# First decay rows copied inside SBUF, VectorE columns and residues in other instructions, and a split copy of the last tile

## The chip, the core and the metric

The kernel runs on one core of a Trainium2 chip. The metric is the device time of one execution in microseconds. Five engines run side by side, each with its own queue of instructions in a fixed order: TensorE (PE; PEld is its weight load), VectorE (DVE), ScalarE (ACT), GpSimd (POOL) and SyncE (SP), which here only issues DMAs. An instruction waits until the semaphores that it needs are set, and what stands behind it on its engine waits with it.

## The reference

```python
# 1. attention with decay: B, H, S, D = 4, 8, 576, 64
scores = scale * np.matmul(q, k.transpose(0, 1, 3, 2))
cum = np.cumsum(np.log(np.clip(f, 0.0001, 1.0)), axis=-1)
scores = np.where(causal, -1000000000.0, scores + cum[:, :, :, None] - cum[:, :, None, :])
attn = softmax(scores); x = attn @ v                # -> (4, 576, 512)
# 2. mixture of 4 attention experts, top 2 by gate
logits = x @ w_gate
for e in range(4):
    q, k, v = x @ wq[e], x @ wk[e], x @ wv[e]
    ye = softmax(causal(scale * q @ k.T)) @ v @ wo[e]
    out += gate(logits, e) * ye
# 3. mixer: u = x + (x^T U V)^T, and a hidden layer of 2048
u = x + h.transpose(0, 2, 1)                         # h = x^T @ U @ V
return u + np.maximum(u @ w_ch1, 0.0) @ w_ch2
```

U, V, w_ch1 and w_ch2 come as 64-bit floats.

## The kernel before

The host only lays the arrays out. The order of the instructions is made while the program is written: each piece of work is a generator that asks for an engine, a buffer or an event, and a greedy planner (class Plan, with planned costs and the priorities PR) always runs the piece that can begin first. Each engine then executes its queue in that order, whatever the true times are. A change of a planned cost, or one more step, can so change the order of all that follows. The DMAs of the program use eight semaphores in turn (DMAHW0 to DMAHW7 in the order's rows): a DMA waits until the one before it on its semaphore has landed.

**Layer 1.** Keys and queries of one head stand in a buffer Y (three buffers). Four more partitions, 64 to 67, hold rows made of the decay sums, so that one f32 matmul gives score plus decay. decay() reads f, takes Ln on ScalarE, sums with a scan on VectorE and splits the sums into two parts (the region rw of w2x, rows of 576). It writes six rows a head to DRAM (aug), 8 heads first, then 24; rows() reads them back into Y for each head. The first heads turn the exponentials with TensorE transposes (into the PSUM banks hid and mm) and copy them out on ScalarE and VectorE (pt); later ones split P into an f16 part and an f16 residue (parts()) and turn them by DMA. A residue is x - hi: on VectorE by one instruction, on GpSimd by another; the planner chooses.

**Scales.** Each tensor is scaled by a power of two. pow2() gets the largest power not above the maximum, as a column of one element on 128 partitions; scales() makes from it the scale s (a reciprocal) and its inverse; times() multiplies columns. These columns all lie in one tile, cols.

**While layer 1 starts,** SP reads wall (weights of layer 2), U, V and w_ch1, w_ch2. The 64-bit words are turned into f32 (x, sg, w2x). fold() multiplies wo into w_ch1 on TensorE in 16 steps (hid<-x,wtr).

**Layer 3.** hidden() makes relu(z w) for 256 rows and 256 columns a step (hid, g), outputs() adds g w_ch2 for two tiles of 128 rows into acc (two PSUM banks, one tile of the program), store() scales a tile with ScalarE into o, which has one buffer (r_o), and SP writes it out:

```python
        o = yield r_o
        yield "act"
        copy_scaled(o, a, iv)
        ...
        yield "sp"
        r_o.free(o, dma(out[t0:t0 + 128, :], o).t)
```

Of the kernel before, what the change touches and what calls it, by code (L numbers as in the profile page):

```python
# [20 lines left out]
KB = 5  # L21
# [14 lines left out]
QUEUE = ('act', 'act', 'sp', 'act')  # L36
ACTDMA = 100
PEN = 30.0
WINDOW = 10240 / 3
# [203 lines left out]
def attn_moe_mixer(ctx: ExitStack, tc: tile.TileContext, qk, v, f, wall, wot, wo, w1, w2, u3, v3, out):  # L243
# [74 lines left out]
    def ts(out_, in_, s1, op0, s2=None, op1=None, rate=0.55):  # L318
        kw = {} if op1 is None else {"op1": op1}
        dve("tensor_scalar", rate=rate, out=out_, in0=in_, scalar1=s1, scalar2=s2, op0=op0, **kw)  # L320

    def tt(out_, a, b, op):
        dve("tensor_tensor", out=out_, in0=a, in1=b, op=op)
# [46 lines left out]
    def scales(name, e, k):  # L370
        s, si = col(f"s_{name}"), col(f"i_{name}")
        ts(si, e, float(2.0 ** -k), ALU.mult)
        recip(s, si)
        return s, si

    def times(name, *xs):
        t = col(name)
        tt(t, xs[0], xs[1], ALU.mult)
        for x in xs[2:]:
            tt(t, t, x, ALU.mult)  # L380
        return t
# [87 lines left out]


    def load_heads():
        for i, key in enumerate(HEADS):
            kind, b, h = key
            if i == 2:
                yield ev("rows of first")
            if kind == 1:
                HY[key] = yield r_Y
                HG[key] = (HY[key],)
                yield QUEUE[1]
                n = count(2, "loaded", key)  # L480
                n.done(dma(HY[key][0:64], qk[b, h].rearrange("t d s -> d t s"), queue(1)).t)
                spawn(rows(n, b * H + h, HY[key]), 0)
            else:
                yield ev("stg", b, h // 2)
                X = yield r_X.of([128, 3, 576], F16, "Xh")
                stg = STG[b, h // 2][64 * (h % 2):64 * (h % 2) + 64]
                HG[key] = (X, X)
                n = count(3, "loaded", key)

                for to, of in ((X[0:64], stg[:, 1:4]), (X[64:128, 1:3], stg[:, 2:4]), (X[64:128, 0], stg[:, 0])):  # L490
                    yield "sp"
                    n.done(dma(to, of).t)
                if h % 2:
                    spawn(stg_free(b, h), 0)
# [6 lines left out]
    def rows(n, i, Y):  # L501
        yield ev("aug", i // H)
        yield ev("rows", id(Y))
        yield QUEUE[0]
        a = aug[i]
        n.done(dma(Y[64:68], bass.AP(tensor=a.tensor, offset=a.offset, ap=[[S, 4], [2 * S, 2], [1, S]]), queue(0)).t)
        if i == 0:
            ev("rows of first").done()
# [133 lines left out]
    def parts(hi, lo, x):  # L642
# [5 lines left out]
        if (yield Any(dve=170 + 1.04 * n, pool=180 + 1.93 * n)) == "dve":  # L648
            tt(lo, x, hi, ALU.subtract)
        else:  # L650
# [61 lines left out]
    def pv_out(kind, b, p, j, bank, pv):  # L712
# [13 lines left out]
        if kind == 2:  # L726
            yield ev("gate", b)
            yield "dve"
            tt(rr, rr, GATE[b][:, :, h], ALU.mult)
            if count(E, "gated", b).n == 1:  # L730
# [114 lines left out]
    def values_gates(b):  # L845
# [44 lines left out]
        yield "dve"  # L890
        tt(gt, gt, eq, ALU.add)
# [4 lines left out]
        tt(lg, lg, top.to_broadcast([128, KB, 4]), ALU.subtract)  # L896
        yield "act"
# [9 lines left out]
        yield "dve"  # L907
        tt(lg, lg, top.to_broadcast([128, KB, 4]), ALU.mult)
        wq = yield r_wq
# [323 lines left out]
    def outputs():  # L1233
        yield ev("wox")
        for b, g in groups:
# [16 lines left out]
            for n in range(8):  # L1252
                yield ev("g", (b, g, n))
                gh, gl = GV.pop((b, g, n))
                for fi in range(2):
                    f_ = 2 * n + fi
                    yield ev("w2", f_)
                    for t in range(2):
                        ts_ = slice(t * 128, t * 128 + 128)
                        yield "pe"  # L1260
                        mm(acc[t], gh[:, fi, ts_], w2s[:, f_, 0, :], False, False)
                        mm(acc[t], gh[:, fi, ts_], w2s[:, f_, 1, :], False, False)
                        mm(acc[t], gl[:, fi, ts_], w2s[:, f_, 0, :], False, f_ == NF - 1)
                r_g[0].free(gh)
                r_g[1].free(gl)
            for t in range(2):
                spawn(store(b, g, t, both, acc[t]), PR['store'])

    def store(b, g, t, both, a):
        off = 64 * b  # L1270
        z0 = g * 256 + t * 128
        yield ev("iv", b)
        iv = IV[b] if z0 >= off else IV[b - 1] if z0 + 128 <= off else IV[b, "mixed"]
        o = yield r_o
        yield "act"
# [8 lines left out]
        t0 = b * 576 - off + z0  # L1284
        yield "sp"
# [3 lines left out]
    def decay():  # L1289
        rw = w2x[:32, 8:17, :].rearrange("p a n -> p (a n)")[:, :8 * S].rearrange("p (r s) -> p r s", s=S)  # L1290
        rr = rw.bitcast(F32R)
        one, ff_, cum = rw[:, 0], rw[:, 6], rw[:, 7]
        yield "sp"
        got = dma(ff_, f)
        yield "dve"
        for r, x in ((0, 1.0), (4, -1.0)):
            nc.vector.memset(rw[:, r:r + 2], x)
            plan.cost += 700
        yield got
        yield "dve"  # L1300
# [147 lines left out]
```

## Time and profile before

| | |
|---|---|
| median of 3 runs | 770.49 us (770.06 to 771.51) |
| span of the profiled execution | 770.45 us (770.5 on the page) |
| PE busy | 680.5 us, 88% |
| DVE busy | 476.2 us, 62% |
| ACT busy | 424.1 us, 55% |
| POOL busy | 231.3 us, 30% |
| mean granted TensorE clock | 0.974 |

The span is that of one execution, from its first to its last instruction; it agrees with the median. The busy times of engines run side by side, so they don't add up. A matmul or a copy on the path counts fully, work beside it not at all.

### The profile page before, as it was taken

The page shows a single profiled execution, that of the slowest core. Times are in us where ns is not written, and L with a number is a line of the kernel's source. Part 1 is how long each engine was busy: PE and PEld are TensorE (multiplying, and loading weights), DVE is VectorE, ACT ScalarE, POOL GpSimd, SP SyncE. Part 2 cuts the span into 40 slices and gives each one's busy share as a digit, 9 for nine tenths or more (in the row PEclk, how much of TensorE's full clock was granted, in tenths as well). Part 3 has the DMA queues.
Part 4 walks back from the last instruction along what each step waited for, and adds up shares of the span by engine and source line. Part 5 has one row for each costly group of instructions (what it writes and reads, how often), then busy time and mean ns, then how long its engine had stood idle before and what let it go on. Part 6 is the DMA issues. An engine that isn't in the chain of part 4 may idle for free.

```text
span 770.5 us, 15644 instructions
## 1 busy us (share of the span) xinstructions
PE 680.5 (88%) x5810; PEld 466.3 (61%) x5810; DVE 476.2 (62%) x1548; ACT 424.1 (55%) x889; POOL 231.3 (30%) x286
## 2 busy tenths in 40 slices
PE   3767898687788999999999989998899999899996
PEld 2556776565555666666566666665667656565653
DVE  5888899999878645666874365668734753111111
ACT  4757798687776843566765254767633562112111
POOL 4124333450447620344433022554410340000000
PEclk9969999799999999999999999999999999999999
DMA  8645457572276742779896249888762770000000
GB/s 222 183 109 134 131 151 200 162 212 50 67 152 126 134 92 47 159 160 166 153 187 127 52 87 188 149 150 163 134 106 51 142 149 19 27 1 28 1 28 27
DMA packets 195135, 89.14 MB, mean 116 GB/s; under 512 B 163700, under 2 KB 183156, under 8 KB 195028
## 3 DMA queue, kind: packets, MB, share of 16 engines
q1 hardware_dynamic: 179572, 72.89, 45.2%
q10 hardware_dynamic: 15488, 15.27, 7.6%
q8 instruction: 45, 0.74, 0.4%
q14 instruction: 30, 0.25, 0.1%
HBM read 35.68 MB, written 5.16 MB: 53 GB/s over the span
## 4 chain that ended last, share of the span: by engine, by line
PE 50%; DVE 22%; ACT 9%; issue 5%; DMA 3%; POOL 3%; ACTq 1%; SPq 0%; DVEq 0%; POOLq 0%
PE acc L261 18%; PE mm L261 16%; PE hid L261 12%; DVE sc L272 5%; PE sp L261 3%; DMA pt<-P 3%; ACT sc L266 3%; DVE pt L272 2%; DVE cols L272 2%; POOL P L284 2%; DVE P L272 2%; ACT P L266 2%; DVE w2x L272 1%; DVE nm L272 1%; DVE rr L272 1%
## 5 line engine op out<-in xcount | busy, mean ns | idle before, releaser
L261 PE MATMUL acc<-w2x,g 128*128 128x512 f16 x768 | 180.3, 379 | 0.0
L284 POOL TENSOR_TENSOR P<-sc,P 128x576 f16<-128x576 f32 (+4 forms) x148 | 115.1, 790 | 202.1 <-ACT P L266 154.7
L261 PEld LDWEIGHTS <-g 128*128 128x128 f16 x864 | 82.7, 98 | 83.9 <-issue 1.0
L266 ACT ACTIVATE sc<-sc,nm 128x576 f32<-128x576 f32 (+4 forms) x190 | 103.2, 556 | 47.8 <-DVE nm L272 44.0
L272 DVE SCALAR_TENSOR_TENSOR g<-hid,g 128x512 f16<-128x512 f32 x72 | 49.6, 689 | 122.8 <-ACT g L266 122.5
L261 PE MATMUL sp<-Y 128*128 128x320 f32 (+4 forms) x344 | 106.7, 424 | 17.1 <-DVE nm L272 10.6
L261 PE MATMUL hid<-z,wfr 128*128 128x256 f16 x864 | 107.7, 273 | 5.8 <-DVE g L272 4.7
L261 PEld LDWEIGHTS <-wfr 128*128 128x128 f16 x864 | 83.7, 98 | 30.1 <-issue 8.9
L266 ACT ACTIVATE g<-hid 128x512 f16<-128x512 f32 x72 | 42.6, 591 | 104.9 <-PE acc L261 76.2
L261 PEld LDWEIGHTS sp<-Y 128*128 128x128 f32 x344 | 57.4, 195 | 47.5 <-DVE nm L272 31.2
L266 ACT ACTIVATE P<-sc 128x320 f16<-128x320 f32 (+4 forms) x164 | 70.3, 457 | 20.3 <-DMA pt<-P 10.2
L261 PE MATMUL mm<-V,pt 128*128 128x65 f16 x2058 | 74.5, 194 | 0.8 <-DVE xn L272 0.4
L261 PEld LDWEIGHTS <-pt 128*128 128x128 f16 x2058 | 70.1, 98 | 2.2 <-DVE xn L272 0.7
L261 PE MATMUL mm<-xt,wall 128*128 128x288 f16 x384 | 52.7, 291 | 2.2 <-DVE stg L272 1.9
L272 DVE CUSTOM_DVE_ANT_0 sc<-sp,mask 128x288 f32<-128x288 f32 (+4 forms) x110 | 45.8, 427 | 9.3 <-POOL P L284 5.7
L261 PE MATMUL hid<-x,wtr 128*128 128x128 f32 x256 | 40.2, 323 | 7.2 <-POOL x L284 4.0
L261 PEld LDWEIGHTS <-wall 128*128 128x128 f16 x384 | 37.9, 99 | 13.3 <-issue 2.5
L284 POOL TENSOR_TENSOR xh<-xn,xh 128x320 f16<-128x320 f32 x31 | 27.4, 885 | 58.8 <-ACT xh L266 56.2
L261 PEld LDWEIGHTS hid<-x,wtr 128*128 128x128 f32 x256 | 37.5, 233 | 10.1 <-POOL x L284 5.9
L261 PE MATMUL sp<-Xh 128*128 128x64 f16 (+2 forms) x192 | 33.1, 284 | 10.9 <-DVE nm L272 9.9
L272 DVE CUSTOM_DVE_ANT_0 sc<-sp,mask,cols 64x64 f32<-64x64 f32 (+4 forms) x80 | 38.6, 489 | 6.4 <-POOL P L284 3.1
L284 POOL TENSOR_TENSOR x<-x,sg 128x512 f32<-128x512 f32 (+2 forms) x19 | 23.1, 1217 | 64.5 <-DVE x L272 54.7
(141 smaller groups left out, 997.5 us busy)
## 6 DMA issues: line engine op xcount, KB each, us to landing
wd<-in_w SPq DMA_DIRECT2D x32, 512.0 KB
Y<-in_qk ACTq DMA_DIRECT2D x32, 288.0 KB
vr<-in_v ACTq DMA_DIRECT2D x16, 320.0 KB
out_dram<-o SPq DMA_DIRECT2D x18, 256.0 KB
Xh<-stg SPq DMA_DIRECT2D x16, 216.0 KB
Xh<-stg SPq DMA_DIRECT2D x16, 144.0 KB
w2x<-in_wall SPq DMA_DIRECT2D x4, 386.0 KB
Xh<-stg SPq DMA_DIRECT2D x16, 72.0 KB
```

Of the source, the lines that this page charges most:

```text
L261: nc.tensor.matmul(out_, lhsT=lhsT, rhs=rhs, start=start, stop=stop, **kw)
L266: nc.scalar.activation(out_, in_, fn, **kw)
L272: getattr(nc.vector, op)(**kw)
L284: getattr(nc.gpsimd, op)(out=out_, **kw)
```

## The change

Five edits:

- rows(): for the first three heads (DIRECT) the decay rows go from the region rw straight to Y, by two DMAs a head of four rows each, with no DRAM between. The other heads read aug as before.
- decay(): a column of ones gets a Ln before f is there, and an Exp behind the real Ln, each with its own table load.
- scales(): s is made by integer arithmetic on the exponent, in one tensor_scalar, ahead of its inverse; the reciprocal goes. times() multiplies by columns given as scalars, two in one instruction.
- parts() and four other places (the gates): a difference or product of two tensors on VectorE is written as scalar_tensor_tensor (times 1.0 first) in place of tensor_tensor.
- outputs() and store(): in the last step of the last group the matmuls of the first tile stand ahead of those of the second, and the first is stored at once. The second is copied in two halves, ScalarE's and VectorE's, into the buffer sc, and each half has its own DMA.

```diff
+DIRECT = 3
+    def stt(out_, a, b, op):
+        dve("scalar_tensor_tensor", out=out_, in0=a, scalar=1.0, in1=b, op0=ALU.mult, op1=op)
     def scales(name, e, k):
         s, si = col(f"s_{name}"), col(f"i_{name}")
+        ts(s.bitcast(I32), e.bitcast(I32), -1.0, ALU.mult, float((254 + k) << 23), ALU.add)
         ts(si, e, float(2.0 ** -k), ALU.mult)
-        recip(s, si)
         return s, si
     def times(name, *xs):
         t = col(name)
-        tt(t, xs[0], xs[1], ALU.mult)
-        for x in xs[2:]:
-            tt(t, t, x, ALU.mult)
+        ts(t, xs[0], xs[1], ALU.mult, *((xs[2], ALU.mult) if len(xs) > 2 else ()))
+        for x in xs[3:]:
+            ts(t, t, x, ALU.mult)
         return t
...
     def rows(n, i, Y):
-        yield ev("aug", i // H)
+        direct = i < DIRECT
+        yield ev("cum") if direct else ev("aug", i // H)
         yield ev("rows", id(Y))
-        yield QUEUE[0]
-        a = aug[i]
-        n.done(dma(Y[64:68], bass.AP(tensor=a.tensor, offset=a.offset, ap=[[S, 4], [2 * S, 2], [1, S]]), queue(0)).t)
+        if direct:
+            for t in range(2):
+                yield QUEUE[0]
+                n.done(dma(Y[64:68, t], CUM[0][i:i + 1, 2 * t:2 * t + 4], queue(0)).t)
+        else:
...
         if (yield Any(dve=170 + 1.04 * n, pool=180 + 1.93 * n)) == "dve":
-            tt(lo, x, hi, ALU.subtract)
+            residue(lo, x, hi)
...
-                for fi in range(2):
+                end = (b, g) == groups[-1] and n == 7
+                for i in range(4):
+                    fi, t = (i % 2, i // 2) if end else (i // 2, i % 2)
...
+                    if end and i == 1:
+                        spawn(store(b, g, t, both, acc[t]), PR['store'])
...
     def store(b, g, t, both, a):
...
+        if (b, g) == groups[-1] and t == 1:
+            o = (yield r_sc[KB - 1])[:, :DM]
+            for engine, to, cs in (("act", nc.scalar, slice(0, DM // 2)), ("dve", None, slice(DM // 2, DM))):
+                yield engine
+                if engine == "act":
+                    copy_scaled(o[:, cs], a[:, cs], iv)
+                else:
+                    ts(o[:, cs], a[:, cs], iv, ALU.mult)
+            for to, cs in ((None, slice(DM // 2, DM)), (nc.scalar, slice(0, DM // 2))):
+                yield "act" if to else "sp"
+                dma(out[t0:t0 + 128, cs], o[:, cs], to)
+            return
...
     def decay():
+        warm = col("warm", 2)
...
+        nc.vector.memset(warm, 1.0)
...
+        yield "act"
+        act(warm[:, 0:1], warm[:, 0:1], ACT.Ln)
         yield got
         yield "dve"
         ts(ff_, ff_, 1e-4, ALU.max, 1.0, ALU.min)
         yield "act"
         act(ff_, ff_, ACT.Ln)
+        yield "act"
+        act(warm[:, 1:2], warm[:, 1:2], ACT.Exp)
...
+        CUM.append(rw)
+        ev("cum").done()
```

At the start of the program ScalarE's queue stood like this before (vr are the values of layer 1, junk the output of an Abs whose sum is kept, sc_97 to sc_99 the first three blocks of the first head, Y_94 to Y_96 the buffers of the first three heads):

```order
L292 DMA vr<-in_v 128x5x128
L266 ACT_TABLE_LOAD
L266 ACTIVATE w2x<-w2x 32x576 [waits DVE_49]
L266 ACTIVATE junk,cols<-vr 128x640 [waits DMAHW3_49]
L266 ACTIVATE junk,cols<-vr 128x640 [waits DMAHW5_49,Activation_49]
L292 DMA Y_94<-aug 4x2x576 [waits DMAHW6_49,DMAHW0_49,Pool_49]
L292 DMA Y_95<-aug 4x2x576 [waits DMAHW1_49,Pool_49]
L292 DMA Y_96<-in_qk 64x2x576 [waits DMAHW2_49]
```

And now, from the read of the second values to the first exps and the copy of U (x<-wd):

```order
L267 ACT_TABLE_LOAD
L267 ACTIVATE cols<-cols 128x1
L267 ACTIVATE junk,cols<-vr 128x640 [waits DMAHW3_49]
L293 DMA Y_94<-w2x 4x1x576 [waits DVE_49,Pool_49]
L293 DMA Y_95<-w2x 4x1x576 [waits DMAHW0_49,Pool_49]
L293 DMA Y_94<-w2x 4x1x576 [waits DMAHW1_49]
L293 DMA Y_95<-w2x 4x1x576 [waits DMAHW2_49]
L267 ACTIVATE junk,cols<-vr 128x640 [waits DMAHW5_49,Activation_49]
L293 DMA Y_96<-w2x 4x1x576 [waits DMAHW6_49]
L267 ACTIVATE sc_97<-sp,nm 64x64 [waits DVE_49]
L267 ACTIVATE sc_98<-sp,nm 128x192 [waits DVE_49]
L267 ACTIVATE x<-wd 128x480 [waits DMAHW7_49]
```

The row DMAs moved ahead of the second Abs, they are two for each head, and the copy of U, which waits for its DMA, stands ahead of the exp of sc_99.

SP's queue, just behind its first two reads, went like this before (aug<-w2x are the DRAM writes of the decay rows, w2x<-in_wall the weights of layer 2, wd<-in_u the read of U):

```order
L292 DMA aug<-w2x 8x3456 [waits DVE_49]
L292 DMA aug<-w2x 24x3456
L292 DMA w2x<-in_wall 128x772 [waits DMAHW3_49]
L292 DMA w2x<-in_wall 128x772 [waits DMAHW4_49]
L292 DMA w2x<-in_wall 128x772 [waits DMAHW6_49]
L292 DMA w2x<-in_wall 128x772 [waits DMAHW7_49]
L292 DMA wd<-in_u 128x960 [waits DMAHW0_49]
```

And now:

```order
L293 DMA aug<-w2x 8x3456 [waits DVE_49]
L293 DMA aug<-w2x 24x3456 [waits DMAHW5_49]
L293 DMA wd<-in_u 128x960 [waits DMAHW7_49]
L293 DMA wd<-in_v 96x576 [waits DMAHW0_49]
L293 DMA w2x<-in_wall 128x772 [waits DMAHW1_49]
```

U moved ahead of the weights; its semaphore DMAHW7 was last used by the first of the two DRAM writes, and DMAHW5 by the second values.

At the end of the program TensorE's last step went, in its middle, like this before (g_9590 and g_9591 are the two parts of the last relu; the first three matmuls shown are the first tile's, the others the second's):

```order
L261 MATMUL acc<-w2x,g_9590 128x512
L261 LDWEIGHTS g_9590
L261 MATMUL acc<-w2x,g_9590 128x512
L261 LDWEIGHTS g_9591
L261 MATMUL acc<-w2x,g_9591 128x512
L261 LDWEIGHTS g_9590
L261 MATMUL acc<-w2x,g_9590 128x512
```

And now, where the first tile's six matmuls are over with the third row and the second tile's begin (the relu's parts are g_9588 and g_9589 here):

```order
L262 MATMUL acc<-w2x,g_9588 128x512
L262 LDWEIGHTS g_9589
L262 MATMUL acc<-w2x,g_9589 128x512
L262 LDWEIGHTS g_9588
L262 MATMUL acc<-w2x,g_9588 128x512 [waits Activation_49]
L262 LDWEIGHTS g_9588
```

The wait for ScalarE in front of the second tile is new. ScalarE ended with these rows before:

```order
L266 ACTIVATE g_9558<-hid 128x512 [waits DVE_49,PE_49]
L266 ACTIVATE g_9574<-hid 128x512 [waits DVE_49,PE_49]
L266 ACTIVATE g_9590<-hid 128x512 [waits DVE_49,PE_49]
L266 ACTIVATE o<-acc,cols 128x512 [waits DMAHW0_49,PE_49]
L266 ACTIVATE o<-acc,cols 128x512 [waits DMAHW1_49,Activation_49]
```

And now:

```order
L267 ACTIVATE g_9572<-hid 128x512 [waits DVE_49,PE_49]
L267 ACTIVATE g_9588<-hid 128x512 [waits DVE_49,PE_49]
L267 ACTIVATE o<-acc,cols 128x512 [waits DMAHW3_49,PE_49]
L267 ACTIVATE sc_101<-acc,cols 128x256 [waits PE_49]
L293 DMA out_dram<-sc_101 128x256 [waits Activation_49]
```

VectorE, whose last row was a relu's residue before, now ends with:

```order
L273 SCALAR_TENSOR_TENSOR g_9528<-hid,g_9527 128x512 [waits PE_49,Activation_49]
L273 SCALAR_TENSOR_TENSOR g_9557<-hid,g_9556 128x512 [waits PE_49,Activation_49]
L273 SCALAR_TENSOR_TENSOR g_9573<-hid,g_9572 128x512 [waits PE_49,Activation_49]
L273 SCALAR_TENSOR_TENSOR g_9589<-hid,g_9588 128x512 [waits PE_49,Activation_49]
L273 TENSOR_SCALAR sc_101<-acc,cols 128x256 [waits Activation_49]
```

The copy of the second tile became two halves, ScalarE's with a DMA of its own, and VectorE's waits for a ScalarE instruction. In TensorE's queue, nothing differs from the first layer-3 matmuls on but for a few pieces that change places, until this last step; ahead of them the pieces of layers 1 and 2 and of the folds stand in another order.

## Rows read from the trace of the kernel before

**Rows 1.** The page, part 1: busy us (share of the span) xinstructions.

```profile
PE 680.5 (88%) x5810; PEld 466.3 (61%) x5810; DVE 476.2 (62%) x1548; ACT 424.1 (55%) x889; POOL 231.3 (30%) x286
```

**Rows 2.** Busy time by stage: stretch, length, each engine's busy time, granted clock, DMA.

```profile
0.00:14.70 14.70, 1.57 (x5) 1.01 (x5) 8.14 (x18) 4.59 (x7) 9.00 (x37) 1.00 0.80 202
14.70:236.70 222.00, 176.35 (x1560) 138.22 (x1561) 193.89 (x571) 168.03 (x361) 79.38 (x70) 0.92 0.55 143
236.70:763.77 527.07, 502.61 (x4247) 327.08 (x4245) 274.23 (x960) 250.12 (x520) 142.87 (x180) 1.00 0.52 102
763.77:770.50 6.73, 0.00 (x0) 0.00 (x0) 0.00 (x0) 1.37 (x2) 0.00 (x0) 0.78 0.21 78
```

**Rows 3.** Timeline of the start: start us, us, engine line op out<-in [idle before <-releaser].

```profile
3.55 1.28 ACT L266 ACT_TABLE_LOAD   x1 [3.55 <-issue]
...
4.84 0.68 ACT L266 ACTIVATE w2x<-w2x 32x576 f32<-32x576 f32 x1
...
7.42 0.75 DVE L272 SCALAR_TENSOR_TENSOR w2x<-w2x 32x576 fp32r<-32x576 f32 x1
...
7.92 0.74 ACT L266 ACTIVATE junk<-vr 128x640 f16<-128x640 f32 x1 [2.39 <-DMA vr<-in_v]
...
8.19 0.68 SPq L292 DMA_DIRECT2D aug<-w2x  x2
...
11.63 0.87 ACTq L292 DMA_DIRECT2D Y<-aug  x2
...
14.67 0.33 SPq L292 DMA_DIRECT2D wd<-in_u  x1
...
14.70 3.99 PE L261 MATMUL sp<-Y 128*128 128x64 f32 x8 [2.49 <-DMA Y<-aug]
...
18.50 0.53 ACT L266 ACTIVATE sc<-sp,nm 128x320 f32<-128x320 f32 x1 [0.26 <-DVE nm L272]
```

**Rows 4.** Groups by form on VectorE, whole run: xcount | busy us, mean ns | idle.

```profile
L272 DVE TENSOR_TENSOR cols<-cols 128x1 f32<-128x1 f32 x47 | 10.0, 220 | 0.8
...
L272 DVE TENSOR_SCALAR cols<-cols 128x1 f32<-128x1 f32 x52 | 7.9, 152 | 1.6
...
L272 DVE RECIPROCAL cols<-cols 128x1 f32<-128x1 f32 x25 | 4.1, 164 | 0.9
```

**Rows 5.** Groups by form on VectorE, 14.7 to 236.7 us.

```profile
L272 DVE TENSOR_TENSOR cols<-cols 128x1 f32<-128x1 f32 x13 | 3.3, 264 | 0.1
```

**Rows 6.** Tile P on VectorE: ns min/median/max, first and last start, forms.

```profile
L272 DVE TENSOR_TENSOR P<-sc,P x22: 611/1330/1396, 218.8 to 630.2; 128x448 f16<-128x448 f32 x16, 128x320 f16<-128x320 f32 x2, 128x192 f16<-128x192 f32 x2, 64x64 f16<-64x64 f32 x1
```

**Rows 7.** Tile w2x on VectorE.

```profile
L272 DVE SCALAR_TENSOR_TENSOR w2x<-w2x,cols x12: 744/752/1196, 212.8 to 275.0; 128x512 f16<-128x512 f32 x12
```

**Rows 8.** Timeline, a residue of w2x and GpSimd beside it.

```profile
270.81 1.28 POOL L284 TENSOR_TENSOR P<-sc,P 128x576 f16<-128x576 f32 x1
...
271.44 1.20 DVE L272 SCALAR_TENSOR_TENSOR w2x<-w2x,cols 128x512 f16<-128x512 f32 x1
```

**Rows 9.** Timeline of the end.

```profile
752.58 11.17 PE L261 MATMUL acc<-w2x,g 128*128 128x512 f16 x51
...
759.02 0.69 DVE L272 SCALAR_TENSOR_TENSOR g<-hid,g 128x512 f16<-128x512 f32 x1 [1.90 <-ACT g L266]
763.79 0.69 ACT L266 ACTIVATE o<-acc,cols 128x512 f32<-128x512 f32 x1 [4.80 <-PE acc L261]
764.50 3.13 SPq L292 DMA_DIRECT2D out_dram<-o  x2
766.59 0.69 ACT L266 ACTIVATE o<-acc,cols 128x512 f32<-128x512 f32 x1 [2.11 <-DMA out_dram<-o]
```

**Rows 10.** The chain that ended last, its last DMA: start us, us, what.

```profile
764.50 2.00 DMA out_dram<-o
```

**Rows 11.** Folds (tile wtr) on PE: stretch, length, busy (x), granted clock, DMA.

```profile
85.00:88.00 3.00, 1.95 (x16) 1.00 0.48 115
...
143.50:148.00 4.50, 3.78 (x16) 0.50 0.53 155
```

More of the change, by code (lines that the diff above doesn't have):

```diff
@@ L467, in attn_moe_mixer @@
     si_w, si_u, i_o, s_wf, s_wo = {}, {}, {}, {}, {}
+    CUM = []
     def load_heads():
@@ L479, in load_heads @@
                 yield QUEUE[1]
-                n = count(2, "loaded", key)
+                n = count(3 if b * H + h < DIRECT else 2, "loaded", key)
                 n.done(dma(HY[key][0:64], qk[b, h].rearrange("t d s -> d t s"), queue(1)).t)
@@ L501, in rows @@
     def rows(n, i, Y):
-        yield ev("aug", i // H)
+        direct = i < DIRECT
+        yield ev("cum") if direct else ev("aug", i // H)
         yield ev("rows", id(Y))
-        yield QUEUE[0]
-        a = aug[i]
-        n.done(dma(Y[64:68], bass.AP(tensor=a.tensor, offset=a.offset, ap=[[S, 4], [2 * S, 2], [1, S]]), queue(0)).t)
+        if direct:
[3 more added lines that the diff above has]
+        else:
+            yield QUEUE[0]
+            a = aug[i]
+            n.done(dma(Y[64:68], bass.AP(tensor=a.tensor, offset=a.offset, ap=[[S, 4], [2 * S, 2], [1, S]]), queue(0)).t)
         if i == 0:
@@ L728, in pv_out @@
             yield "dve"
-            tt(rr, rr, GATE[b][:, :, h], ALU.mult)
+            stt(rr, rr, GATE[b][:, :, h], ALU.mult)
             if count(E, "gated", b).n == 1:
@@ L890, in values_gates @@
         yield "dve"
-        tt(gt, gt, eq, ALU.add)
+        stt(gt, gt, eq, ALU.add)
         yield "dve"
@@ L895, in values_gates @@
         yield "dve"
-        tt(lg, lg, top.to_broadcast([128, KB, 4]), ALU.subtract)
+        stt(lg, lg, top.to_broadcast([128, KB, 4]), ALU.subtract)
         yield "act"
@@ L907, in values_gates @@
         yield "dve"
-        tt(lg, lg, top.to_broadcast([128, KB, 4]), ALU.mult)
+        stt(lg, lg, top.to_broadcast([128, KB, 4]), ALU.mult)
         wq = yield r_wq
@@ L1254, in outputs @@
                 gh, gl = GV.pop((b, g, n))
-                for fi in range(2):
+                end = (b, g) == groups[-1] and n == 7
+                for i in range(4):
+                    fi, t = (i % 2, i // 2) if end else (i // 2, i % 2)
                     f_ = 2 * n + fi
                     yield ev("w2", f_)
[L1258 to L1263, printed above, removed]
+                    ts_ = slice(t * 128, t * 128 + 128)
+                    yield "pe"
+                    mm(acc[t], gh[:, fi, ts_], w2s[:, f_, 0, :], False, False)
+                    mm(acc[t], gh[:, fi, ts_], w2s[:, f_, 1, :], False, False)
+                    mm(acc[t], gl[:, fi, ts_], w2s[:, f_, 0, :], False, f_ == NF - 1)
+                    if end and i == 1:
+                        spawn(store(b, g, t, both, acc[t]), PR['store'])
                 r_g[0].free(gh)
                 r_g[1].free(gl)
-            for t in range(2):
+            for t in range(1 if end else 0, 2):
                 spawn(store(b, g, t, both, acc[t]), PR['store'])
@@ L1273, in store @@
         iv = IV[b] if z0 >= off else IV[b - 1] if z0 + 128 <= off else IV[b, "mixed"]
+        t0 = b * 576 - off + z0
+        if (b, g) == groups[-1] and t == 1:
[10 more added lines that the diff above has]
+            return
         o = yield r_o
@@ L1283, in store @@
                 r_acc.free(both, n.t)
-        t0 = b * 576 - off + z0
         yield "sp"
```

## The prediction

> **What bounds the kernel now.** I first read the busy times of the whole run [rows 1]: TensorE 680.5 of 770.5 us. An average over unlike stages says little, so I cut the span at three events: the first score matmul (14.70), the first matmul of the hidden layer (236.7) and the last matmul (763.77) [rows 2]. Four stages appear. In the first 14.7 us TensorE works 1.57 us: a stage of waiting for the first operands. From 14.7 to 236.7 TensorE is busy 176 of 222 us at a mean granted clock of 0.92, and VectorE is the fullest engine (194 us). From 236.7 to the last matmul TensorE is busy 503 of 527 us. The last 6.7 us hold two ScalarE copies and output DMAs. So time can be taken at the two ends and in the second stage; in the third, VectorE and GpSimd time is mostly covered by matmuls. The compared orders of TensorE support this cut: they differ in the second stage and hardly behind it, so what is won or lost before about 237 us is carried to the end.
>
> **The start.** The timeline [rows 3] shows the chain: Ln on ScalarE from 4.84 (behind a table load of 1.28 us), the sums done on VectorE at 7.42 + 0.75 = 8.17, the write to DRAM issued at 8.19, the read back issued at 11.63, the first score matmul at 14.70. The new path has no DRAM write. On ScalarE the row DMAs now stand behind one Abs that started when its values had landed, 7.92; two issues took 0.87 there, so the first head's second DMA, third in the queue, is issued near 7.92 + 0.87 = 8.8. With the old distance from issue to matmul, 14.70 - 11.63 = 3.07, scores begin at 11.9: 2.8 us earlier. The early table loads cost nothing: the first runs beside the DMA of f and its clamp, the second is covered by the wait for the values. Without that cover it is 1.28 us.
>
> But the change adds a wait. U is now read ahead of the weights on SP, and its DMA uses the semaphore of the first DRAM write: issued no sooner than that write lands, about 8.19 to 11.63. Its 480 KB (128 x 960 words) at the 202 GB/s of this stage [rows 2] need 2.4 us, plus 2.0 from issue to landing of an output DMA [rows 10]: about 16. On ScalarE the copy of U now stands ahead of the exp of the first head's third block (18.50 before), and behind it wait that head's transposes and VectorE. So the gain there is rather 2 us than 2.8. I take 2.0, between 2.8 (U lands in time) and nothing (it lands 2.4 us later than my estimate).
>
> **Residues as scalar_tensor_tensor.** VectorE makes 23 residues of P and one of xh in the new order. A TENSOR_TENSOR of P took 611 ns at best, 1330 at the median [rows 6]; the form with a scalar took 744 at best and 752 at the median for 512 columns, with f32 and f16 operands as here [rows 7]. By columns that is the same price. The long cases are waits for GpSimd: at 271.44 the form with a scalar took 1.20 us and ended 0.55 us behind a GpSimd operation that ended at 272.09 [rows 8]. The new form therefore waits as well, and I cost the swap at nothing; so too the few small ones of the gates.
>
> One rule speaks against the change. The Trainium skill, Vector Engine (DVE) Microarchitecture Reference, section "7. Points that are easy to get wrong", says that scalar_tensor_tensor with two SBUF sources that aren't bf16 halves its throughput. These residues are such, and by that rule they would lose (a rival below); the 752 ns of this trace don't look like half rate, though no row shows both instructions on one shape. By the row the sum below stands; by the rule it would be some 8 us more.
>
> **Columns without reciprocal.** On columns of one element, 47 TENSOR_TENSOR take 220 ns in the mean, TENSOR_SCALAR 152, RECIPROCAL 164 [rows 4]. 41 of the 47 become 33 TENSOR_SCALAR, and 24 reciprocals become TENSOR_SCALAR. Eight fewer instructions are 8 x 0.22 = 1.8 us, the 33 others give up 33 x 0.07 = 2.3 at most (waits for GpSimd raise their mean; TENSOR_SCALAR shows none), the reciprocals 24 x 0.01 = 0.3: at most 4.4 us of VectorE time. What counts is the second stage, where VectorE is full: 13 TENSOR_TENSOR of 264 ns there [rows 5], 13 x 0.11 = 1.5 us. I take 1.5, with bounds of 0 (those waits pass to the next instruction with two SBUF operands) and 4.4.
>
> **The end.** Now the last matmul ends at 763.75, ScalarE copies from 763.79 to 764.48, its DMA is issued at 764.50 and lands 2.0 later [rows 10], the second copy waits for the buffer until 766.59 and ends at 767.28; 3.17 us follow to the end [rows 9]. The change puts the second tile into another buffer and halves its copy, so the wait of 2.1 us goes. Two waits come, and the new order shows both. The first matmul of the second tile waits for ScalarE, and behind the relu of the last hidden tile, already waited for, the only ScalarE instruction is the first tile's copy: TensorE, which ran without a break, stands still for the start (0.03, as before the copy at 763.79), the copy of 0.69 and the way back (taken as 0.03), 0.75 in all, before its last six matmuls. And the VectorE half waits for ScalarE's half. A half lies between 0.35 and the 0.69 us of a whole copy on either engine [rows 9]; with 0.5: 763.75 + 0.75 + 0.5 + 0.5 + 3.17 = 768.7, or 1.7 us earlier. With whole prices it is 769.1 (1.4 us); were neither wait real, 763.8 + 0.5 + 3.17 = 767.5 (3.0 us).
>
> **The order of the second stage.** The faster start moves every planned time, and the same greedy planner orders stage two anew. The work is equal; idle time isn't. Its price is best seen on the folds of w1: 16 matmuls took 1.95 us at full granted clock and 3.78 at 0.50, that is at 1.2 instead of 2.4 GHz [rows 11]. I count no gain or loss, and two batches either way, 3.7 us, as a bound.
>
> **The sum.** The profiled execution spans 770.45 us, against a median of 770.49, so nothing is added around it. 770.45 - 2.0 - 1.5 - 1.7 = 765.25: I predict 765.3 us.
>
> **The rivals.** *The early gain is lost in stage two*: VectorE has 28 us of idle time there to swallow it, and the later weights (their DMAs now wait for the rows) could hold it. Then only the end is left, with some of the columns: 770.45 - 1.7 - 0.5 = 768.3. For it speaks the wait for U; against it that VectorE is the fullest engine and gets the same work sooner.
>
> *The new order costs more than it saves*: TensorE stands still more often, and the clock falls in more of the batches. Each costs 1.8 us [rows 11]; from three it cancels the 5.2 us of gains, with five the time is 765.3 + 9 = 774. For it speaks that the clock fell in that stage already (0.92 in the mean); against it that VectorE, which the matmuls there mostly wait for, has no more to do.
>
> *The new order saves as much again*: three dear batches become cheap: 765.3 - 5.5 = 760.
>
> *The residues do not wait for GpSimd*: 22 residues of P spend up to 1.33 - 0.61 = 0.72 us each in waits, 16 us at most, a quarter of it on the path in the third stage: 765.3 - 4 = 761. The 1.20 us row speaks against it.
>
> *The residues run at half rate*: at most another 0.66 us each (752 x 448 / 512), 24 x 0.66 = 16 us, half on the path: 773. The 752 ns speak against it: 1.47 ns per column with all fixed cost, where the best TENSOR_TENSOR has 611 / 448 = 1.36. This is the rule of the Trainium skill cited with the residues.
>
> **How the numbers follow.** The forecast (763 to 767.5) has 0.45, the lost early gain 0.20, the dear order 0.14, the cheap order 0.12, residues without waits 0.04, at half rate 0.03; 0.02 for anything else. 768.95 is the line for 0.2%, about what a measurement of this kernel can tell from no change. The lost gain (768.3, give or take 1) lies two thirds below it; of the dear order a fifth ends within 0.2% and the rest above. Faster: 0.45 + 0.13 + 0.12 + 0.04 = 0.74. Same: 0.07 + 0.03 = 0.10. Slower: 0.11 + 0.03 + 0.02 = 0.16. The range leaves out most of the dear order and half rate (0.12) and the tail of the cheap order (0.06): 758.5 to 771.0.
>
> **What would show it.** Start: first score matmul near 11.9, the copy of U near 16, that third exp near 16.5. Residues of P: the new instruction at 600 to 1400 ns, with the same waits. Columns: no TENSOR_SCALAR over 0.2 us. End: a gap of about 0.75 us ahead of the last six matmuls, VectorE's half behind ScalarE's, 4.2 us from the last matmul to the end. Stage two: first hidden matmul near 233, and a mean clock near 0.92. I am wrong if that first hidden matmul doesn't come earlier, or if the third stage, its new gap aside, changes by over a microsecond.

## The result: slower, by the new order of stage two

The changed kernel took 780.84 us in the median (778.05 to 784.14, four runs) beside 771.0 (770.06 to 771.85) for the kernel before: a ratio on record of 1.0104, 95% interval 1.0075 to 1.0134 (the quotient of the two medians alone would be 1.0128, inside that interval). I had predicted 765.3 us and a range up to 771.0. The profiled execution spans 777.9 us.

The page of the changed kernel, part 1, to be read beside [rows 1]:

```profile
PE 678.6 (87%) x5810; PEld 466.5 (60%) x5810; DVE 474.9 (61%) x1544; ACT 423.9 (54%) x889; POOL 232.5 (30%) x287
```

No engine has much more to do: GpSimd has 1.2 us more, and TensorE has the same 5810 matmuls and 1.9 us less busy time. So the time must be idle time, and the question is where. The windows, cut at the same events as [rows 2] (first score matmul, first matmul of the hidden layer, last matmul):

```profile
core 0: us, PE busy (x) PEld busy (x) DVE busy (x) ACT busy (x) POOL busy (x), PEclk, DMA share, GB/s
0.00:13.66 13.66, 0.77 (x3) 0.54 (x3) 7.09 (x13) 4.37 (x7) 8.47 (x37) 1.00 0.77 185
13.66:243.16 229.50, 173.58 (x1555) 136.54 (x1555) 191.82 (x571) 168.80 (x361) 80.52 (x69) 0.92 0.54 138
243.16:774.23 531.07, 504.23 (x4254) 329.47 (x4253) 275.52 (x960) 250.30 (x521) 143.52 (x182) 1.00 0.53 103
774.23:777.90 3.67, 0.00 (x0) 0.00 (x0) 0.48 (x1) 0.47 (x1) 0.00 (x0) 1.00 0.22 77
```

The first stage is 1.0 us shorter, the last 3.1 shorter, stage two 7.5 longer and the third 4.0. So both signs by which the prediction said that it would be wrong have come: the first hidden matmul is later (243.16 us for 236.7), and the third stage, its new gap of 0.78 us aside, grew by 3.2 us. A cleaner cut for the third stage is the first matmul that adds a relu's part to acc (acc<-w2x,g), at 252.59 us before and 263.58 now. Before:

```profile
14.70:252.59 237.89, 190.11 (x1712) 147.88 (x1713) 205.40 (x606) 179.23 (x383) 89.75 (x80) 0.92 0.56 143
252.59:763.77 511.18, 488.84 (x4100) 317.42 (x4096) 262.71 (x924) 238.91 (x499) 132.51 (x170) 1.00 0.52 101
```

And the changed kernel:

```profile
13.66:263.58 249.92, 190.76 (x1716) 148.90 (x1717) 206.76 (x621) 183.60 (x390) 92.70 (x82) 0.92 0.55 138
263.58:774.23 510.65, 487.05 (x4094) 317.10 (x4093) 260.58 (x912) 235.50 (x491) 131.34 (x169) 1.00 0.52 101
```

From that event on the two are alike (511.2 and 510.7 us). Ahead of it TensorE works 190.1 and 190.8 us at the same mean granted clock, 0.92, but the stretch takes 249.9 in place of 237.9: TensorE stands 59.2 us instead of 47.8. Nearly all that is lost, and more than start and end won, is idle time of TensorE between 14 and 264 us: 3.5 us of the 11.4 ahead of 140 us, 7.9 behind it.

**The start,** timeline of the changed kernel, as [rows 3]:

```profile
4.33 0.67 ACT L267 ACTIVATE w2x<-w2x 32x576 f32<-32x576 f32 x1
...
6.89 0.75 DVE L273 SCALAR_TENSOR_TENSOR w2x<-w2x 32x576 fp32r<-32x576 f32 x1
...
7.72 1.20 ACTq L293 DMA_DIRECT2D Y<-w2x  x1
...
9.02 3.20 ACTq L293 DMA_DIRECT2D Y<-w2x  x3
...
11.28 0.36 SPq L293 DMA_DIRECT2D wd<-in_u  x1
...
13.66 2.47 PE L262 MATMUL sp<-Y 128*128 128x64 f32 x6 [3.98 <-DMA Y<-w2x]
...
17.91 0.63 ACT L267 ACTIVATE x<-wd 128x480 f32<-128x480 f32 x1 [1.93 <-DMA wd<-in_u]
18.45 0.51 ACT L267 ACTIVATE sc<-sp,nm 128x320 f32<-128x320 f32 x1
```

The early table load moved Ln from 4.84 to 4.33 us. The first row DMA goes out at 7.72 and takes 1.20 us to issue, and the next three take the queue from 9.02 to 12.22. In the order each of these three waits for an older DMA on its semaphore, the first for none; how much of the 3.20 us is such a wait was not measured. Scores start 1.0 us earlier in this execution, and the third exp, which stands behind the copy of U, starts at 18.45 (18.50 before). U came at 17.9, not at 16. For that exp the gain of the start was gone.

**Stage two.** What TensorE waited for from 140 to 264 us (engine, what for, us in total, times, longest; the longest rows), before:

```profile
PE sp L261 <- DVE nm L272: 8.8, 14, 2.1
PE mm L261 <- DVE stg L272: 3.5, 4, 1.6
PE hid L625 <- DVE pt L272: 2.8, 5, 1.1
PE hid L261 <- POOL x L284: 2.3, 1, 2.3
...
```

And the changed kernel in the same stretch:

```profile
PE sp L262 <- DVE nm L273: 7.2, 9, 1.7
PE mm L262 <- DVE stg L273: 6.0, 3, 2.1
PE hid L262 <- DVE z L273: 2.2, 1, 2.2
PE mm L262 <- DVE th L273: 2.2, 1, 2.2
PE mm L262 <- DVE cols L273: 1.7, 4, 0.7
...
```

Most lines are waits that VectorE ends, in both; nm is what VectorE takes from a block of scores for its exp. New are longer waits for stg (the staged queries and keys of layer 2), th and z (the mixer). VectorE was not slower: it came later to these pieces. A staging is two instructions, ScalarE's copy and then VectorE's residue, which reads that copy. The timeline of both at one of these waits, in which TensorE stands 2.15 us, up to 168.17, for the stg of 167.67:

```profile
164.55 1.47 DVE L273 SCALAR_TENSOR_TENSOR wfr<-wfr,cols 128x512 f16<-128x512 f32 x1 [0.29 <-ACT wfr L267]
...
165.95 0.41 DVE L273 TENSOR_SCALAR w2x<-w2x 128x512 int32<-128x512 int32 x1
...
166.14 0.70 ACT L267 ACTIVATE wfr<-wfr,cols 128x512 f16<-128x512 f32 x1
166.40 0.69 DVE L273 SCALAR_TENSOR_TENSOR w2x<-wd,w2x 128x512 int32<-128x512 int32 x1
166.75 0.39 ACT L267 ACTIVATE stg<-mm 128x288 f16<-128x288 f32 x1
167.00 0.75 DVE L273 SCALAR_TENSOR_TENSOR wfr<-wfr,cols 128x512 f16<-128x512 f32 x1
...
167.67 0.45 DVE L273 SCALAR_TENSOR_TENSOR stg<-mm,stg 128x288 f16<-128x288 f32 x1
```

Weight preparation (w1 scaled in wfr, w2 converted in w2x) stands ahead of the staging on both engines. The residue could not start before ScalarE's copy ended at 167.14, and that copy stood behind a scaling of w1 on ScalarE; VectorE's own last piece of preparation then held it to 167.67. So of the 2.15 us 1.1 pass until ScalarE's copy is done, 0.5 are VectorE's queue and 0.45 the residue itself. The first batch's last stg started at 173.5 before and starts at 188.1 now.

**The residues and the columns,** by form over the whole run, beside [rows 6] and [rows 4]:

```profile
L273 DVE SCALAR_TENSOR_TENSOR P<-sc,P 128x448 f16<-128x448 f32 x17 | 22.7, 1338 | 23.9 <-ACT P L267 23.9
L273 DVE TENSOR_SCALAR cols<-cols 128x1 f32<-128x1 f32 x85 | 14.7, 177 | 1.2
L273 DVE TENSOR_SCALAR cols<-cols 128x1 int32<-128x1 int32 x44 | 6.8, 154 | 1.6
L273 DVE TENSOR_TENSOR cols<-cols 128x1 f32<-128x1 f32 x6 | 0.9, 151 | 0.0
```

The 128x448 residues take 1338 ns in the mean where they took 1219, with other neighbours in the new order. Of the 25 reciprocals of columns one is left, and the products of columns moved to TENSOR_SCALAR.

**The end** went as forecast, as [rows 9]:

```profile
772.04 0.69 ACT L267 ACTIVATE o<-acc,cols 128x512 f32<-128x512 f32 x1 [3.50 <-PE acc L262]
...
772.77 1.46 PE L262 MATMUL acc<-w2x,g 128*128 128x512 f16 x6 [0.78 <-ACT o L267]
774.27 0.47 ACT L267 ACTIVATE sc<-acc,cols 128x256 f32<-128x256 f32 x1 [1.54 <-PE acc L262]
...
774.77 0.48 DVE L273 TENSOR_SCALAR sc<-acc,cols 128x256 f32<-128x256 f32 x1 [5.52 <-ACT sc L267]
```

TensorE stands 0.78 us for the first tile's copy, VectorE's half starts as ScalarE's ends, and 3.67 us follow the last matmul.

### The profile page after: what moved, and what is told of

It is laid out like the page before. It is cut to its first block, busy times and chain, and to the rows that moved or that the text cites. A ratio compares the mean times of both kernels' runs of the same rounds, so it can differ in the third digit from the quotient of the medians.

```text
span 777.9 us, 15661 instructions
## 1 busy us (share of the span) xinstructions
PE 678.6 (87%) x5810; PEld 466.5 (60%) x5810; DVE 474.9 (61%) x1544; ACT 423.9 (54%) x889; POOL 232.5 (30%) x287
## 5 line engine op out<-in xcount | busy, mean ns | idle before, releaser
L285 POOL TENSOR_TENSOR P<-sc,P 64x64 f16<-64x64 f32 (+4 forms) x147 | 113.2, 781 | 202.4 <-ACT P L267 158.2
L262 PE MATMUL sp<-Y 128*128 128x320 f32 (+4 forms) x344 | 108.8, 433 | 20.2 <-DVE nm L273 11.6
L262 PEld LDWEIGHTS sp<-Y 128*128 128x128 f32 x344 | 59.4, 202 | 48.1 <-DVE nm L273 27.8
L267 ACT ACTIVATE P<-sc 128x192 f16<-128x192 f32 (+4 forms) x163 | 69.8, 456 | 20.6 <-DMA pt<-P 7.2
L262 PE MATMUL hid<-x,wtr 128*128 128x128 f32 x256 | 36.2, 301 | 11.0 <-DVE pt L273 4.1
L273 DVE SCALAR_TENSOR_TENSOR P<-sc,P 128x448 f16<-128x448 f32 (+4 forms) x23 | 28.7, 1247 | 26.3 <-ACT P L267 26.2
L262 PEld LDWEIGHTS hid<-x,wtr 128*128 128x128 f32 x256 | 33.8, 212 | 15.5 <-POOL x L285 9.3
```

The source lines that it names most:

```text
L262: nc.tensor.matmul(out_, lhsT=lhsT, rhs=rhs, start=start, stop=stop, **kw)
L267: nc.scalar.activation(out_, in_, fn, **kw)
L273: getattr(nc.vector, op)(**kw)
L285: getattr(nc.gpsimd, op)(out=out_, **kw)
```

## The experiments

The theory after this reading: no instruction is dear; the loss is the order that the planner made from the edits. The main rivals: an instruction is dear by itself, or the direct rows hurt by their DMAs. Medians of the kernel before lay between 771 and 775 us on different occasions, so all runs are told as ratios to the kernel before run beside them, with 95% intervals; 0.1% is 0.8 us.

### One part at a time

Each kernel is the kernel before with one part of the change, its diff cut out of the one shown ahead of the prediction. In the first only the instructions differ, in the last only the end; columns and start also lead to another order.

```diff
 e1_stt
-            tt(lo, x, hi, ALU.subtract)
+            residue(lo, x, hi)
...
 e1_cols
+        ts(s.bitcast(I32), e.bitcast(I32), -1.0, ALU.mult, float((254 + k) << 23), ALU.add)
...
-        recip(s, si)
...
 e1_start
...
+                n.done(dma(Y[64:68, t], CUM[0][i:i + 1, 2 * t:2 * t + 4], queue(0)).t)
...
 e1_end
...
+                    fi, t = (i % 2, i // 2) if end else (i // 2, i % 2)
...
```

> The kernel before, with only the residues of P and xh and the four small gate operations on VectorE written as scalar_tensor_tensor; TensorE's, ScalarE's, GpSimd's and SyncE's orders are those of before. Order theory (the loss comes from the new order of stage two, no instruction is dearer): 771.0, within 0.2% of before, residues of P with a mean near 1220 to 1250 ns. Rival, dear instructions (scalar_tensor_tensor at a lower rate on the path): 774 to 781, residues well above 1400 ns.

Measured: 0.9992 (0.9975 to 1.001). The residues, with the order unchanged:

```profile
L272 DVE SCALAR_TENSOR_TENSOR P<-sc,P x22: 628/1329/1397, 220.0 to 633.9; 128x448 f16<-128x448 f32 x16, 128x320 f16<-128x320 f32 x2, 128x192 f16<-128x192 f32 x2, 64x64 f16<-64x64 f32 x1
```

Least, median and greatest are those of [rows 6] within 17 ns, and no effect on the time shows. The long ones wait for GpSimd, in both forms. One and the same residue, before and in e1_stt:

```profile
318.14 1.28 POOL L284 TENSOR_TENSOR P<-sc,P 128x576 f16<-128x576 f32 x1 [1.27 <-ACT P L266]
318.56 1.34 DVE L272 TENSOR_TENSOR P<-sc,P 128x448 f16<-128x448 f32 x1 [1.27 <-ACT P L266]
```

```profile
319.77 1.28 POOL L284 TENSOR_TENSOR P<-sc,P 128x576 f16<-128x576 f32 x1 [1.27 <-ACT P L266]
320.19 1.34 DVE L272 SCALAR_TENSOR_TENSOR P<-sc,P 128x448 f16<-128x448 f32 x1 [1.27 <-ACT P L266]
```

Both end 0.48 us behind GpSimd's instruction. So do 15 of the 16 residues of 128x448 before and all 16 of e1_stt; the one left, of 611 ns, started with GpSimd's and ended first.

> The kernel before, with only the scales without reciprocal and the products of columns as tensor_scalar; the order is that of before up to about the 2380th instruction of TensorE and differs in pieces behind it. Order theory: a small number either way, 768 to 774, whose sign is set by the pieces that change places; by the instructions alone 769.5. Rival, the integer scales are dear: over 774, with some column instruction of over 0.3 us on the chain.

Measured: 1.0153 (1.01 to 1.0206), far more than I expected of either sign, and enough for the rival. With the next part, two and not one lose over 1% each when they are alone.

> The kernel before, with only the first three heads' decay rows from SBUF to SBUF and the early table loads; order of stages one and two made anew, third stage as before. Order theory: most of the loss is here, 777 to 783, with the first hidden matmul near 243 and the first score matmul near 13.7. Rival, instruction prices: 769 to 771 (the early rows give up to 1 us).

Measured: 1.0121 (1.0061 to 1.018); first score matmul at 14.45 us, first hidden matmul at 241.18. The loss is where the changed kernel has it: from the first score matmul to the first acc<-w2x,g TensorE stands 57.8 us here. And in the two traces TensorE's instructions follow each other in the same sequence up to 250.6 us. So TensorE's order in stage two of the changed kernel is the one that the planner made from the start's edit.

> The kernel before, with only the split evacuation of the last group; order otherwise as before. Both theories: 768.5 to 769.3, from 3.7 us behind the last matmul in place of 6.7, less a stand of 0.78 us ahead of its last six matmuls.

Measured: 0.998 (0.9962 to 0.9998): 1.5 us, with 0.2 to 2.9 inside the interval; the sum had 1.7.

### Edit and order apart

The planner takes its order from costs that the program tells it. So the new instructions can be put in the order of before, by telling the old costs, and the old instructions in the new order. By the names in the traces, TensorE's sequence in e2_cols_cost, e2_start_old and e2_all_old is that of before from end to end, and in e2_cols_order that of e1_cols.

```diff
 e2_cols_cost: new columns, old order
+        plan.cost += 75 * min(len(xs) - 2, 1)
 e2_cols_order: old columns, new order
+        plan.cost -= 75 * min(len(xs) - 2, 1)
 e2_start_old: direct rows emitted where the read of aug stood, planned as that one read
...
+        if i < DIRECT:
+            for t in range(2):
+                queue(0).dma_start(out=Y[64:68, t], in_=CUM[0][i:i + 1, 2 * t:2 * t + 4])
+            src = None
+        n.done(dma(Y[64:68], src, queue(0)).t)
```

> The kernel before with the new scales and products of columns, while the planner is told the old costs: the instructions are new, the order on all engines is that of before. Order theory: 0.997 to 1.001 of before (768.5 to 771.3 where before takes 770.5). Rival, the new column instructions are dear by themselves: near the 1.015 of the run with new instructions and new order.

Measured: 0.9982 (0.9957 to 1.0006).

> The kernel before with its old scales and products of columns, while the planner is told the costs of the new ones: old instructions, and the order on all engines that the new columns gave. Order theory: 1.010 to 1.020 of before (778 to 786 where before takes 770.5), with TensorE standing and at half clock in the third stage as with the new columns. Rival, dear instructions: 1.000.

Measured: 1.0222 (1.0189 to 1.0255). The instructions are word for word those of before; the order alone costs 2.2%, somewhat above the range that I gave. The rival is out. Windows of this kernel, cut as above:

```profile
14.90:249.87 234.97, 186.21 (x1713) 144.55 (x1714) 204.39 (x606) 179.51 (x384) 91.07 (x81) 0.94 0.56 144
249.87:777.69 527.82, 492.48 (x4100) 319.17 (x4096) 263.78 (x925) 240.37 (x500) 129.17 (x167) 1.00 0.51 98
```

Here the loss lies elsewhere than in the changed kernel: stage two is even shorter than before (235.0 us against 237.9), but in the third TensorE stands 35.3 us in place of 22.3, and works 3.6 us longer. What it waited for there, from 252 to 764 us, before:

```profile
PE sp L261 <- DVE nm L272: 12.3, 22, 1.2
PE hid L261 <- DVE g L272: 4.7, 7, 2.0
...
```

and with the columns' order:

```profile
PE sp L261 <- DVE nm L272: 17.1, 30, 1.9
PE hid L261 <- DVE g L272: 11.3, 12, 3.1
...
```

> The kernel before with the three heads' decay rows from SBUF to SBUF and the early table loads, while the planner is told of one old read for each head: TensorE, VectorE, GpSimd and SyncE keep the order of before, and on ScalarE the row DMAs stand where the reads stood. Order theory: 0.996 to 1.000 of before, first score matmul 12.5 to 13.7. Rival, the direct rows hurt by themselves (DMA semaphores shared with U and the weights): 1.008 or more.

Measured: 1.0029 (1.0014 to 1.0044), first score matmul at 15.28. Between the two: the direct rows, with the early tables, lose 2 us in this order, a quarter of what this part alone lost; the rest of its 1.0121 is order. Where the 2 us go isn't shown: TensorE's idle time in stage two is 48.4 us, as before, and the first row DMA goes out only at 10.08, since the rows stand behind the second Abs here.

> All five edits, with the order of before up to the last step of the last group (the planner is told the old costs). Order theory: 0.993 to 0.998 of before (765 to 769 where before takes 770.5), first hidden matmul at or before 236.7. Rival, dear instructions or start: 1.005 or more, as the changed kernel's 1.010.

Measured: 0.9965 (0.995 to 0.998), and in stage two the idle time of before (235.88 less 187.84 is 48.0):

```profile
14.88:250.76 235.88, 187.84 (x1712) 146.12 (x1713) 203.05 (x604) 177.96 (x382) 88.82 (x80) 0.93 0.57 145
```

All five edits together are 2.7 us faster than before; with the order that they lead to, 8 us slower. The order's price is 1.0104 / 0.9965 = 1.014, about 10.7 us, give or take 2.5 by the two intervals.

TensorE's idle time, up to the first acc<-w2x,g and from there to the last matmul, repeats well where the order is the same: in the nine kernels of this document that keep the order of before it is 44.3 to 48.4 us in stage two and 22.3 to 24.6 in the third. Its busy time in stage two differs by more between their profiled executions, 185.8 to 192.0 us, at mean granted clocks of 0.93 and 0.91. So one profile against one other can mislead by several us; the ratios rest on 4 to 12 runs each.

### Is any new order dear?

Two kernels with the instructions of before, in which the planner is told a cost that no edit of the change has (in e3_draw2 the products of columns cost it more, where the change made them cost less):

```diff
 e3_draw1
     def decay():
+        plan.cost += 1000
 e3_draw2, in times()
+        plan.cost += 75
```

> The kernel before, instruction for instruction, but the planner is told that the decay work costs 1 us more: another order of stages one and two, no edit of the change in it. Theory that any replan of this kernel costs about as much as the changed one (the order of before is a picked one): 1.006 to 1.02 of before. Rival, only the planner's view of the change is bad and other orders are as good as that of before: 0.997 to 1.003.

Measured: 1.002 (1.0 to 1.004), below the theory's range and within the rival's. In the profiled execution TensorE stands 54.4 us in stage two, but its busy time there is low (186.9 us at a mean clock of 0.94).

> The kernel before, instruction for instruction, but the planner is told that each product of columns costs 75 ns more (where the change told it 75 ns less). Theory that any replan costs: 1.006 to 1.02 of before. Rival, shorter columns alone lead to bad orders: 0.997 to 1.003.

Measured: 1.0335 (1.0311 to 1.0359). So an order can be nearly free or more than twice as dear as that of the change (3.35% against 1.4%), and 75 ns told otherwise for each product are enough. In draw2 TensorE stands 56.7 us in stage two and 32.8 in the third.

### One suspect moved

The trace had shown the scaling of w1 between the stagings. The changed kernel, with that scaling (on ScalarE and VectorE) asked to wait:

```diff
 g_gate, in wf_scaled() ahead of the splits
+        for p in range(2):
+            yield count(4, "stg", 0, p)
```

> The changed kernel with one line more: the scaling of w1 is not started before the first batch's layer-2 projections are staged (stg); the planner orders all behind it anew. Theory that the w1 scaling between the stagings on VectorE is what delays layer 2: last staging of the first batch before 180 us (188 in the changed kernel), first acc matmul with w2x at 258 or earlier (263.6), time 0.996 to 1.004 of before. Rival, the loss is spread over many pieces and this one is nothing special: last staging near 188 still or the loss back at another place, 1.007 to 1.02.

Measured: 1.0346 (1.0302 to 1.039). The waits for stg fell, in the stretch from 140 to 266 us, from 6.0 us to:

```profile
...
PE mm L262 <- DVE stg L273: 3.0, 2, 1.9
...
```

and TensorE stands 55.4 us in stage two in place of 59.2. But the last staging of the batch still began at 185.5, and the first acc matmul with w2x came at 265.35, in part because the first score matmul came only at 17.89. And its third stage takes 528.5 us instead of 510.7, TensorE standing 37.1 us of it (23.6 in the changed kernel). My theory of one guilty piece falls: moving it won back 3.7 of the 11.4 us of idle time in stage two, and the order that followed lost more in the third.

### The start and the end mended

```diff
 e3_start_old1: as e2_start_old
+DIRECT = 1
 e3_best1: new columns and split end, order of before, and
+                if (b, g) == groups[-1] and t == 1:
+                    a = (yield r_hid).rearrange("p a n -> p (a n)")
...
+            oa = (yield r_sc[KB - 1])[:, :DM // 2]
+            od = (yield r_sc[KB - 2])[:, :DM // 2]
 g_best2: e3_best1 and e3_start_old1 together
```

> The early table loads, and SBUF to SBUF rows for the first head alone (two row DMAs in place of six), in the order of before. Theory that the direct rows lose by the number of DMAs, each waiting for an older DMA on its semaphore: first score matmul at 13.7 or earlier (15.28 with six), time 0.998 to 1.001 of before. Rival, the path through SBUF is no earlier by itself: first score matmul near 15.3, time 1.002 to 1.004.

Measured: 0.9991 (0.9972 to 1.0009), first score matmul at 14.40. The time is in the theory's range, the matmul isn't: two direct DMAs do not lose, and no gain is shown. In the kernels with the old start the first score matmul came between 14.70 and 15.71.

> The order of before, new columns, old start and old residues, and the split end with its two waits removed: the second tile's accumulator in a bank of its own (that of the hidden layer, unused by then), and the two halves in two buffers. Theory that the two waits of the split end are only shared tiles: no stand ahead of the last six matmuls, 3.2 us from the last matmul to the end, 0.994 to 0.996 of before (the columns 0 to 0.2%, the end 2.5 to 3 us). Rival, the half copies or the DMAs behind them wait for something else: 0.996 to 0.998, as with the end as it is.

Measured: 0.9932 (0.991 to 0.9955), just below the theory's range. The end of this kernel, the second tile now in the bank hid:

```profile
761.46 1.46 PE L261 MATMUL hid<-w2x,g 128*128 128x512 f16 x6
761.66 0.69 ACT L266 ACTIVATE o<-acc,cols 128x512 f32<-128x512 f32 x1 [3.50 <-PE acc L261]
...
762.95 0.47 ACT L266 ACTIVATE sc<-hid,cols 128x256 f32<-128x256 f32 x1 [0.61 <-PE hid L261]
...
763.46 0.48 DVE L272 TENSOR_SCALAR sc<-hid,cols 128x256 f32<-128x256 f32 x1 [4.58 <-ACT sc L266]
```

TensorE no longer stands, so that wait was the shared tile. From the last matmul to the end 3.9 us pass, not 3.2. VectorE's half still begins when ScalarE's ends, though the two now write into two buffers, so that wait isn't the output's. Both halves still read one tile, and whether that is its cause was not tried.

> The order of before with the new columns, the early table loads, direct rows for the first head alone, and the split end without its two waits. If the parts add: 0.991 to 0.994 of before (0.9932 without the start, 0.9991 for the start alone). Rival, the early start is lost in stage two in this combination: 0.993 to 0.996.

Measured: 0.9924 (0.9899 to 0.9949), 767.78 us in the median beside 774.29: the fastest version here, some 6 us below the kernel before on the same chip, though not clear of e3_best1. Its first score matmul comes at 14.67, so the start can't be seen to add to it.

## Why the prediction was wrong

**The step that failed** is "the order of the second stage", which I put at no gain or loss, with 3.7 us either way as a bound. The new order costs 10.7 us (1.4%), shown by the same edits in the two orders, and the idle time says that it costs them in stage two. That the start would make the planner order this stage anew was right (e1_start); two things in the price were wrong. I bounded it by the clock, two batches of folds at half rate [rows 11], but the mean granted clock of the stretch did not change in the two profiles (0.92); what changed was the time that TensorE stands, most of it until VectorE is done, 59.2 us against 47.8. And I took the two signs as alike. My rival of a dear order (774 us, a chance of 0.14) had the right side and, in "TensorE stands still more often", the right half of its mechanism; it too took its price from the clock. Against it I had put that VectorE has no more to do. That is true (its busy time in the prediction's stage two fell from 193.9 to 191.8 us) and says nothing: the same work, in another order, makes TensorE wait longer.

**The start** (-2.0) was mis-sized: 1.0 us at the first score, none at the third exp, and in the order of before the direct rows with the early tables lose 2.2 us (1.0029). Even the 1.0 us is one execution: with the same rows and tables the first score came at 14.45 in e1_start and 17.89 in g_gate, against 14.70 to 15.71 with the old start. I took an old distance from issue to matmul and counted on the third DMA being issued at 8.8; the queue was still issuing the second to fourth between 9.02 and 12.22. My lower bound of no gain held for the changed kernel's third exp, not for the edit by itself.

**The columns** (-1.5): 0.9982, that is -1.4, with no effect still inside the interval. Busy time in the forms of [rows 4] with the integer ones fell by 2.5 us: 10.0 + 7.9 + 3.1 + 4.1 = 25.1 before, 14.7 + 6.8 + 0.9 and one reciprocal of 0.2 = 22.6 after. No TENSOR_SCALAR was to take over 0.2 us; 33 of the 85 do, as many as there are products of columns given as scalars: 0.20 to 0.27 us each, in e2_cols_cost as well, while the other 52 stay under 0.16. And the mean of 220 ns that I set them against was made by six long ones of up to 1.08 us; the median of the 47 was 159 ns. So a product itself became dearer, not cheaper by 0.07 us; what was saved is the eight instructions and the long ones.

**The residues** (0): 0.9992, the durations those of before. The rule of the Trainium skill, Vector Engine (DVE) Microarchitecture Reference, section "7. Points that are easy to get wrong", by which this form would run at half rate, isn't borne out beside TENSOR_TENSOR: 628 ns at best against 611, and 0.48 us from the end of GpSimd's instruction in both forms. That row also answers the rival of residues that do not wait: they wait as before, as the prediction had read it.

**The end** (-1.7): 0.998, that is -1.5, inside its interval, with both new waits where I had read them: 0.78 us for 0.75, halves of 0.47 and 0.48 us for 0.5. After the last matmul came 3.67 us where I had 4.2.

**The cut into stages** was placed too early: of the loss, 4.5 us lie between the first hidden matmul and the first acc<-w2x,g (15.9 us before, 20.4 now), which the prediction counted to the third stage. From that event on the third stage keeps what it is handed, in this order (510.7 against 511.2 us). It isn't general: in e2_cols_order and g_gate the third stage grew by 17 us.

The four parts measured one by one in the order of before add up to some -1.3 us (+2.2, -1.4, -0.6, -1.5), the five edits together to -2.7; their intervals, over 1 us either way each, allow it. The forecast of -5.2 was too high even without the order, mostly by the start.

**What stays open:** which pieces of the new order cost the 11 us, and which step of the start's edit led the planner to it. The piece that I moved was not decisive, and moving a piece makes the planner order all that follows anew. Of the new orders here (the changed kernel, the start, the columns, two draws and the gate) none is shown to be faster than the one of before: they stand 0.2 to 3.5% above it; that the order of before had been picked among many would explain it, but is only argued.

## What to carry to other kernels

Where a planner makes the order from costs, an edit has two prices: that of its instructions and that of the order it leads to. Tell the planner the old costs and measure the edit in the old order first; here that turned 1.0% slower into 0.35% faster, and with the start cut to one head and TensorE's wait at the end taken away (and the residues left as they were) into 0.76%. When a prediction must price a new order unseen, don't write zero with two equal sides: take the idle time of the engine that bounds the stage (TensorE's 48 of 238 us here, which became 54 to 59 in five of the six new orders) as what can move. That the worse side is the likelier one is borne out only by the six new orders tried here.

## What was not expected

- The small DMAs inside SBUF were not quick to issue here: four row DMAs of 9 KB took ScalarE's queue from 7.72 to 12.22 us, where two reads of 18 KB from DRAM had taken 0.87 [rows 3].
- The start varies by itself. In g_gate, whose first stage has the same instructions in the same order as the changed kernel, the first score matmul came at 17.89 us instead of 13.66. The read of weights that waits on the semaphore of the first head's second row DMA (DMAHW1 in the order's rows) went out at 17.81 instead of 13.58, so that DMA seems to have landed 4 us later.
- A planned cost changed by 75 ns for each of some products of columns changed the time of the kernel by 17 us (e2_cols_order) and 25 us (e3_draw2), with every instruction the same.
